# Dense experts' first product by seven block products, in an attention and two mixture-of-experts kernel

## The chip, the core and the metric

The kernel runs on one core of a Trainium2 chip. The core has five engines with queues of their own: TensorE (PE in the profile; its weight loads are PEld), VectorE (DVE), ScalarE (ACT), GpSimd (POOL) and SyncE (SP), which issues most transfers. TensorE multiplies a weight tile of 128 x 128 with up to 512 moving columns and adds into an accumulation bank (PSUM); the other operands lie in on-chip memory (SBUF). Engines wait for each other by semaphores. The metric is the device time of one execution in microseconds.

## What is computed

Attention with rotated positions (2 batches, 8 heads, 576 positions, head size 64) gives x, 1,152 tokens of 512 values. A first layer of 8 experts follows, of which each token takes its two best (routed experts), and then a second layer in which every token goes through all 4 experts (dense experts). The change is in the dense experts:

```python
def _moe2_ref(x, domain_probs, w1, w2) -> np.ndarray:
    N, D = x.shape                       # 1152, 512
    E = w1.shape[0]                      # 4; w1 is E x 512 x 1024, w2 is E x 1024 x 512
    p = domain_probs / (domain_probs.sum(-1, keepdims=True) + 1e-09)
    out = np.zeros((N, D), dtype=np.float32)
    for e in range(E):
        h = np.maximum(x @ w1[e], 0.0)   # the first product
        out += p[:, e:e + 1] * (h @ w2[e])   # the second product
    return out.astype(np.float32)
```

## The kernel before

**Numbers in two parts.** Every large operand is kept as a high part, rounded to the type that TensorE multiplies fast, and a low part, the difference. A product a x b is three products: high x high, low x high and high x low. `wchunk` (L94) loads a weight chunk of 128 x 512 as `raw` (five buffers), lets one engine cast the high part (L99 on ScalarE) and another subtract the low part (L102), both into one tile, `w1c` for first weights and `w2c` for second ones (eight buffers each).

**Stages.** Attention runs to about 190 us, with products of 288 columns (`av`, L392, and `ps_s`, L321). Then the routing is worked out, and the eight routed experts run in the loop at L789, each on up to 320 gathered tokens: first product `ps_h` (L804), ReLU on ScalarE (`hh`, L805), low part on VectorE (`hl`, L806), second product `ps_y` (L866), copy to `yt`, transpose `pt_y` (L835). Outputs are written to `yd` in memory; those of the last expert are added to x2 at once (L841).

**Between the layers.** x2, the dense experts' input, has nine tiles of 128 tokens. For each tile `fetch` (L713) issues two gathers from `yd` on GpSimd's queue (L722), `combine` (L726) adds both to x2 on VectorE (L729), and `turn_x2` (L733) transposes the tile on TensorE (L736) and splits it into `xh2` and `xl2` (L112, L113). The tables `fetch_at` and `combine_at` (L775) put tiles 0 to 2 into the last routed expert; tiles 3 to 8 follow between the first products of the first dense expert, with `raw` buffers for the gathered rows.

**Dense experts.** The loop at L899 takes the four experts in turn. The first product goes by hidden block f (eight of 128) and token group t (three of 384): 12 matmuls of 384 columns into one of three banks (L922), a ReLU into `h2h` on ScalarE (L923) and a low part into `h2l` on VectorE (L924). Then the second product takes 24 matmuls of 512 columns per token tile (L937), and VectorE adds each tile, times its probability, to the accumulator (L940 for the first expert, L942 for the others), which after the last expert leaves by a put on GpSimd's queue (L946). Second weights are loaded and split in the first product, first weights of the next expert in the second one; ScalarE casts and GpSimd subtracts.

**What sets the order.** A scheduler orders the instructions of each engine, largely as they are written; `issue_after` holds one behind another. Each engine then works through its queue in order.

Of the kernel before, what the change touches and what calls it, by code (L numbers as in the profile page):

```python
# [15 lines left out]
P = 128  # L16
# [11 lines left out]
def tile_attention_moe_moe(  # L28
# [65 lines left out]
    def wchunk(src, pool, tag, hi, lo):  # L94
        raw = rawp.tile([P, 512], F32, tag="raw", name="raw")
        nc.sync.dma_start(raw if len(src.shape) == 2 else raw.rearrange("p (k f) -> p k f", k=KC), src)
        t = pool.tile([P, 2, 512], F32R, tag=tag, name=tag)
        if hi is nc.scalar:
# [4 lines left out]
        return t  # L103

    def w1chunk(src, f, hi, lo):
        return wchunk(src[:, f * P:(f + 1) * P].rearrange("(k p) f -> p k f", p=P), w1p, "w1c", hi, lo)
# [400 lines left out]
    psg = ctx.enter_context(tc.tile_pool(name="psg", bufs=3, space=PSUM))  # L507
    psy = ctx.enter_context(tc.tile_pool(name="psy", bufs=2, space=PSUM))
    pstr = ctx.enter_context(tc.tile_pool(name="pstr", bufs=2, space=PSUM))
# [104 lines left out]
    y_writes, y_adds = [], []  # L614
# [98 lines left out]
    def fetch(c):  # L713
        for k2 in range(2):
            i = 2 * c + k2
            if c > 2:
                ygs[i] = rawp.tile([P, DM], F32, tag="raw", name="yg")
            else:
                if i % 3 == 0:
                    yg = gx.tile([P, 3, DM], F32, tag="g", name="yg")  # L720
# [68 lines left out]
    for e in range(E1):  # L789
# [4 lines left out]
        for f in range(FC):  # L794
# [28 lines left out]
            if e == LAST:  # L823
                last_steps(f)
# [6 lines left out]
        def turn_y(d, yt, yn, e=e):  # L831
# [5 lines left out]
            if e == LAST:  # L837
                for j in range(NJ):
                    n = min(P, CAP - j * P)
                    c = NT - full + j if j < full else NT - NJ  # L840
                    y_adds[:] = [vec.scalar_tensor_tensor(  # L841
                        x2[0:n, c, dd], pt[0:n, j * P:(j + 1) * P], tp[0:n, c, 4:5], x2[0:n, c, dd],
                        op0=ALU.mult, op1=ALU.add)]
# [15 lines left out]
        for d in range(KC):  # L859
            for f in (2 * d, 2 * d + 1):  # L860
# [30 lines left out]
    uc1 = {0: wc1}  # L891
# [3 lines left out]
    hh = x2p.tile([P, FC, NT * P], F32R, name="h2h")  # L895
    hl = x2p.tile([P, FC, NT * P], F32R, name="h2l")
    acc = x2
    puts = []
    for e in range(E2):  # L899
        wc1 = uc1.pop(e)  # L900

        if e == 0:
            order = [(f, t, 3) for t in (0, 3, 6) for f in range(FC)]
        else:
            order = [(f, t, 3) for f in range(FC) for t in (0, 3, 6)]
        wc2 = []
        for i, (f, t, m) in enumerate(order):
            if e == 0 and i < 12:
                if i % 2 == 0:
                    with tc.issue_after(y_adds[0].ins):  # L910
                        fetch(i // 2 + 3)
                        combine(i // 2 + 3)
                else:
                    turn_x2(i // 2 + 3)
            if i % (len(order) // FC) == 0:
                wc2.append(w2chunk(u2[e], len(wc2), nc.scalar, nc.gpsimd))
            o = slice(t * P, (t + m) * P)
            ps = psg.tile([P, 512], F32, tag="g1", name="ps_h2")[:, 0:m * P]
            w = wc1[f].rearrange("p s (k f) -> p s k f", k=KC)
            for n, (s, xx, kk) in enumerate(  # L920
                    [(s, xh2, kk) for kk in range(KC) for s in (0, 1)] + [(0, xl2, kk) for kk in range(KC)]):
                nc.tensor.matmul(ps, w[:, s, kk, :], xx[:, kk, o], start=(n == 0), stop=(n == 3 * KC - 1))  # L922
            nc.scalar.activation(hh[:, f, o], ps, AF.Relu)  # L923
            vec.scalar_tensor_tensor(hl[:, f, o], ps, 0.0, _f(hh[:, f, o]), op0=ALU.max, op1=ALU.subtract)  # L924
        if e + 1 < E2:
            uc1[e + 1] = []
        for c in range(NT):
# [82 lines left out]
```

## Time and profile before

| | us |
|---|---|
| median of three runs | 895.47 (893.74 to 895.69) |
| profiled execution | 893.92 |
| its span, from the first to the last instruction | 892.1 |
| attention and routing | about 200 |
| routed experts | about 275, to 475 |
| dense experts | 475 to 884 |

The profile is of one execution. Busy time is that of an engine's instructions; matmuls overlap, so a matmul's duration is longer than the distance to the next one, and it is the distance, or a stretch divided by its matmuls, that gives the price. The granted clock (PEclk) is 1.00 at 2.4 GHz and 0.5 at 1.2 GHz. The chain of waits follows the work that ended last back through what released it.

### The profile page before, as it was taken

What the parts mean: (1) busy time and instruction counts of PE and PEld (TensorE: products, weight loads), DVE (VectorE), ACT (ScalarE), POOL (GpSimd) and SP (SyncE); (2) the same over time, 40 slices, a digit from 0 to 9 for tenths busy, and PEclk for the clock granted to TensorE, in tenths of its full rate; (3) what the DMA queues carried; (4) which work ended last, traced back from release to release, by engine and by line L of the source; (5) the groups of instructions that cost most, each with busy time, mean ns of one, the idle gap of its engine ahead of it and who ended that gap; (6) DMA issues with size and microseconds to landing.
All of it is one profiled execution on the core that took longest, in us unless ns stands there. A gap on an engine that the chain in (4) does not pass through costs nothing. (4 is left out here: it accounts for less than half of the span.)

```text
span 892.1 us, 13550 instructions
## 1 busy us (share of the span) xinstructions
PE 837.3 (94%) x5148; PEld 780.3 (87%) x5148; DVE 409.1 (46%) x796; ACT 345.0 (39%) x771; POOL 343.9 (39%) x299
## 2 busy tenths in 40 slices
PE   4899999938979989999999899999999999999996
PEld 3799999938979989999999898899888998899885
DVE  7988888867455435446566521122111221122111
ACT  3778888734325345446432440033103330032100
POOL 6768774647455425334045340052104220040011
PEclk9999999978999989999999999999999999999998
DMA  5423231617446465465373420041103210010011
GB/s 147 112 69 96 70 82 41 181 56 246 144 136 187 141 200 152 141 215 173 116 220 102 136 80 15 0 119 38 34 1 85 58 36 12 1 36 1 12 48 47
DMA packets 94636, 84.42 MB, mean 95 GB/s; under 512 B 14036, under 2 KB 74852, under 8 KB 94564
## 3 DMA queue, kind: packets, MB, share of 16 engines
q1 hardware_dynamic: 89204, 69.34, 26.8%
q0 software_dynamic: 4384, 13.47, 4.7%
q8 instruction: 43, 0.70, 0.3%
q10 hardware_dynamic: 976, 0.66, 0.2%
q14 instruction: 29, 0.24, 0.1%
HBM read 69.66 MB, written 9.66 MB: 89 GB/s over the span
## 5 line engine op out<-in xcount | busy, mean ns | idle before, releaser
L937 PE MATMUL ps_y<-w2c,h2h 128*128 128x512 f32 (+1 forms) x592 | 182.4, 389 | 0.0
L922 PE MATMUL ps_h<-xh,w1c 128*128 128x384 f32 x768 | 149.8, 337 | 3.1 <-DVE h2l L924 3.1
L102 POOL TENSOR_TENSOR w2c<-raw,w2c 128x512 fp32r<-128x512 f32 x60 | 83.0, 1409 | 164.8 <-ACT w2c L99 164.7
L922 PEld LDWEIGHTS ps_h<-xh,w1c 128*128 128x128 f32 x768 | 134.0, 188 | 4.6 <-DVE h2l L924 4.3
L937 PEld LDWEIGHTS ps_y<-w2c,h2h 128*128 128x128 f32 x592 | 110.2, 188 | 25.3
L102 POOL TENSOR_TENSOR w1c<-raw,w1c 128x512 fp32r<-128x512 f32 x60 | 77.3, 1293 | 130.9 <-ACT w1c L99 127.8
L866 PE MATMUL ps_y<-hh,w2c 128*128 128x320 f32 x512 | 124.8, 323 | 2.0 <-PEq L742 2.0
L99 ACT CAST w2c<-raw 128x512 fp32r<-128x512 f32 x96 | 56.4, 619 | 174.3 <-issue 133.6
L937 PE MATMUL ps_y<-w2c,h2l 128*128 128x512 f32 (+1 forms) x296 | 115.2, 389 | 0.0
L924 DVE SCALAR_TENSOR_TENSOR h2l<-ps_h,h2h 128x384 fp32r<-128x384 f32 x96 | 53.3, 557 | 134.5 <-ACT h2h L923 134.5
L923 ACT ACTIVATE h2h<-ps_h 128x384 fp32r<-128x384 f32 x96 | 47.0, 492 | 122.0 <-PE ps_h L922 121.0
L804 PE MATMUL ps_h<-xh,w1c 128*128 128x320 f32 x512 | 89.4, 317 | 3.1 <-DVE hl L806 3.1
L866 PEld LDWEIGHTS ps_y<-hh,w2c 128*128 128x128 f32 x512 | 90.2, 195 | 2.2 <-issue 2.2
L866 PE MATMUL ps_y<-hl,w2c 128*128 128x320 f32 x256 | 82.0, 320 | 3.2 <-DVE x L729 1.7
L804 PEld LDWEIGHTS ps_h<-xh,w1c 128*128 128x128 f32 x512 | 79.4, 193 | 3.9 <-DVE hl L806 3.6
L922 PE MATMUL ps_h<-xl,w1c 128*128 128x384 f32 x384 | 82.4, 336 | 0.0
L942 DVE SCALAR_TENSOR_TENSOR x<-ps_y,tp,x 128x512 f32<-128x512 f32 (+1 forms) x28 | 20.5, 732 | 129.5 <-PE ps_y L937 129.5
L922 PEld LDWEIGHTS ps_h<-xl,w1c 128*128 128x128 f32 x384 | 67.9, 188 | 0.0
L937 PEld LDWEIGHTS ps_y<-w2c,h2l 128*128 128x128 f32 x296 | 55.6, 188 | 12.6
L99 ACT CAST w1c<-raw 128x512 fp32r<-128x512 f32 x88 | 54.2, 616 | 13.6 <-DMA raw<-in_moe_w_dram 13.0
L866 PEld LDWEIGHTS ps_y<-hl,w2c 128*128 128x128 f32 x256 | 50.1, 196 | 4.0 <-DVE x L729 2.0
L293 DVE TENSOR_REDUCE nm<-ps_s 128x1 f32<-128x576 f32 x64 | 48.2, 753 | 10.9 <-PE ps_s L321 10.3
(213 smaller groups left out, 1367.6 us busy)
## 6 DMA issues: line engine op xcount, KB each, us to landing
raw<-in_moe_w_dram SPq DMA_DIRECT2D x192, 256.0 KB
Cs<-C SPq DMA_DIRECT2D x28, 144.0 KB
yd<-yn SPq DMA_DIRECT2D x7, 512.0 KB
xd<-xp SPq DMA_DIRECT2D x4, 576.0 KB
vv<-in_v_dram SPq DMA_DIRECT2D x8, 256.0 KB
qk<-in_q_dram SPq DMA_DIRECT2D x7, 256.0 KB
qk<-in_k_dram SPq DMA_DIRECT2D x7, 256.0 KB
yd<-yn SPq DMA_DIRECT2D x7, 128.0 KB
```

Of the source, the lines that this page charges most:

```text
L99: hi.copy(t[:, 0, :], raw)
L102: lo.tensor_sub(t[:, 1, :], raw, _f(t[:, 0, :]))
L293: nc.vector.reduce_max(un.nm[:, c:c + 1], ps[:, :, 0:HS], axis=AX.XY, negate=True)
L804: nc.tensor.matmul(ps, w[:, s, kk, :], xx[:, kk, :], start=(n == 0), stop=(n == 3 * KC - 1))
L866: nc.tensor.matmul(ps, wc2[f][:, s, d * P:(d + 1) * P], xx[:, f, :], start=(n == 0), stop=(n == 3 * FC - 1))
L922: nc.tensor.matmul(ps, w[:, s, kk, :], xx[:, kk, o], start=(n == 0), stop=(n == 3 * KC - 1))
L923: nc.scalar.activation(hh[:, f, o], ps, AF.Relu)
L924: vec.scalar_tensor_tensor(hl[:, f, o], ps, 0.0, _f(hh[:, f, o]), op0=ALU.max, op1=ALU.subtract)
L937: nc.tensor.matmul(ps, xx[:, f, c * P:(c + 1) * P], wc2[f][:, s, dd], start=(n == 0), stop=(n == 3 * FC - 1))
L942: vec.scalar_tensor_tensor(acc[:, c, dd], ps, tp[:, c, 8 + e:9 + e], acc[:, c, dd], op0=ALU.mult, op1=ALU.add)
```

## The change

Experts 1 to 3 get their first product by seven block products in place of eight. The contraction (512), the hidden columns (1,024) and the tokens (1,152) are each halved. For hidden block m and its partner m + 4 (a unit), the four blocks of the weights and four of x give seven products of sums of blocks, with a contraction of 256 and 576 tokens, and the four results are sums of these. Each expert is cut into two sets of two units; a set's four hidden blocks go through the second product at once, which so adds to the accumulator twice as often, with half the matmuls each time.

The sums of x (`T1`, `T2`, `T4` in `Th` and `Tl`; `T3` over a quarter of `xh2` and `xl2`) are formed once, on VectorE and ScalarE, in the first dense expert, which keeps the plain first product. The sums of weights are formed per unit by `unit_weights`, four subtractions of low parts and four half-size additions on GpSimd, in the second product before. The products go to three buffers of two banks (`psu`), for which the pools `psg` and `pstr` are closed. The results are put together on VectorE, partly back into those buffers. A class `InOrder` keeps TensorE, VectorE and ScalarE in the written order from the second half of the first dense expert on. The gathers for tiles 4 to 8 go to temporaries of the dense stage (`tmp`, four buffers) in place of `raw`; tile 3 moves into the last routed expert, and the combines there are held behind the last low part (`last_low`).

```diff
@@ fetch, last_steps @@
-            if c > 2:
-                ygs[i] = rawp.tile([P, DM], F32, tag="raw", name="yg")
+            if c > 3:
+                ygs[i] = temp().rearrange("p j t -> p (j t)")[:, 0:DM]
...
-    fetch_at = {3: (0,), 4: (1,), 5: (2,)}
-    combine_at = {7: (0,), 8: (1,), 9: (2,)}
+    fetch_at = {3: (0,), 4: (1,), 5: (2,), 6: (3,)}
+    combine_at = {7: (0,), 8: (1,), 9: (2,), 10: (3,)}
...
         for c in combine_at.get(i, ()):
-            combine(c)
+            with tc.issue_after(last_low[0]):
+                combine(c)
@@ the dense experts; the loop of L893 to L952 is replaced @@
+    def temp():
+        return x2p.tile([P, 2, TQ], F32, tag="tmp", name="tmp", bufs=4)
...
+    def unit_weights(ra, rb):
+        eng = nc.gpsimd
+        lo, hi = slice(0, 256), slice(256, 512)
+        ta, tb = (split_chunk(x, w1p, "w1c", act, eng) for x in (ra, rb))
+        eng.tensor_tensor(rb[:, hi], rb[:, lo], rb[:, hi], op=ALU.add)
+        eng.tensor_tensor(rb[:, lo], ra[:, lo], rb[:, lo], op=ALU.subtract)
+        eng.tensor_tensor(ra[:, lo], rb[:, hi], ra[:, lo], op=ALU.subtract)
+        eng.tensor_tensor(ra[:, hi], ra[:, hi], ra[:, lo], op=ALU.subtract)
+        tc_, td_ = (split_chunk(x, w1p, "w1c", act, eng) for x in (ra, rb))
...
+    def unit(m, blocks, between):
+        def product(a, b):
+            ps = psu.tile([P, 2, 512], F32, tag="u", name="ps_u")[:, :, 0:TQ]
+            w = blocks[a].rearrange("p s (k f) -> p s k f", k=2)
+            bh, bl = B[b]
+            todo = [(w[:, s, kk], xx[:, kk]) for s, xx in ((0, bh), (1, bh), (0, bl)) for kk in range(2)]
+            for n, (x, y) in enumerate(todo):
+                for j in range(2):
+                    pe.matmul(ps[:, j], x, y[:, j * TQ:(j + 1) * TQ], start=(n == 0), stop=(n == len(todo) - 1))
+            return ps
+
+        def add(ps, other, dst=None):
+            dst = ps if dst is None else dst
+            dve.tensor_tensor(dst, ps, other, op=ALU.add)
+            return dst
+
+        p1 = temp()
+        act.copy(p1, product("11", "11"))
+        between()
+        both = add(product("S2", "T2"), p1, temp())
+        c11 = add(product("12", "21"), p1)
+        relu_hi(2 * m, h0, c11)
+        between()
+        relu_lo(2 * m, h0, c11)
+        v = add(product("S1", "T1"), both, temp())
+        p7 = product("S3", "T3")
+        add(p7, both, both)
+        c22 = add(p7, v)
+        relu_hi(2 * m + 1, h1, c22)
+        c12 = add(product("S4", "22"), v)
+        relu_hi(2 * m, h1, c12)
+        relu_lo(2 * m + 1, h1, c22)
+        relu_lo(2 * m, h1, c12)
+        c21 = add(product("22", "T4"), both)
+        relu_hi(2 * m + 1, h0, c21)
+        relu_lo(2 * m + 1, h0, c21)
+
+    def second(e, s, wc2, cs, after=()):
...
+                todo = [(part, xx, f) for f in (0, 1, 3, 2) for part, xx in ((0, hs[0]), (0, hs[1]), (1, hs[0]))]
...
+    def join(c):
+        combine(c)
+        if c + 2 < NT:
+            fetch(c + 2)
...
+        else:
+            nxt = sets[n + 1] if n + 1 < len(sets) else None
+            for m in range(MS):
+                unit(m, units.pop(m), lambda: split_w2(nc.gpsimd))
+                if m == 0:
+                    load_w2(2, nxt)
+            order = [*range(5, NT), *range(5)]
+            second(e, s, w2s[e, s], order, [lambda x=x: [f() for f in x] for x in make])
```

Here `between` casts and subtracts one chunk of second weights; `h0` and `h1` are the token halves. InOrder's operations all carry the line of its helper, L931 in the new file.

TensorE, first product of expert 1, before: the first three of the expert's 24 groups, each of 8 + 4 matmuls (`ps_h` is the accumulation bank).

```order
L922 MATMUL ps_h_13278<-xh_2638,w1c 128x384 x8
L922 MATMUL ps_h_13278<-xl_2639,w1c 128x384 x4
L922 MATMUL ps_h_13293<-xh_2638,w1c 128x384 x8
L922 MATMUL ps_h_13293<-xl_2639,w1c 128x384 x4
L922 MATMUL ps_h_13308<-xh_2638,w1c 128x384 x8
L922 MATMUL ps_h_13308<-xl_2639,w1c 128x384 x4
```

TensorE, the same place now: the seven products of a unit begin with these (`ps_u` is a buffer of two banks, `Th` and `Tl` the parts of the sums of x).

```order
L931 MATMUL ps_u<-xh_2638,w1c 128x288 x8
L931 MATMUL ps_u<-xl_2639,w1c 128x288 x4
L931 MATMUL ps_u<-Th,w1c 128x288 x8
L931 MATMUL ps_u<-Tl,w1c 128x288 x4
L931 MATMUL ps_u<-xh_2638,w1c 128x288 x8
L931 MATMUL ps_u<-xl_2639,w1c 128x288 x4
```

Behind every 12 matmuls of 384 columns stood a ReLU and a low part; now each 12 of 288 columns are one product, and VectorE has this between two sets of accumulations (all eleven operations of a unit are these).

```order
L931 TENSOR_TENSOR tmp<-ps_u,tmp 128x576
L931 TENSOR_TENSOR ps_u<-ps_u,tmp 128x2x288
L931 SCALAR_TENSOR_TENSOR h2l<-ps_u,h2h 128x576
L931 TENSOR_TENSOR tmp<-ps_u,tmp 128x576 x2
L931 TENSOR_TENSOR ps_u<-ps_u,tmp 128x2x288 x2
L931 SCALAR_TENSOR_TENSOR h2l<-ps_u,h2h 128x576 x2
L931 TENSOR_TENSOR ps_u<-ps_u,tmp 128x2x288
L931 SCALAR_TENSOR_TENSOR h2l<-ps_u,h2h 128x576
```

VectorE, the last routed expert, before: combines (`x<-yg`) between the last three low parts (`hl`).

```order
L729 SCALAR_TENSOR_TENSOR x_2634<-yg,tp,x_2634 128x512
L806 SCALAR_TENSOR_TENSOR hl<-ps_h,hh 128x320
L729 SCALAR_TENSOR_TENSOR x_2634<-yg,tp,x_2634 128x512 x2
L806 SCALAR_TENSOR_TENSOR hl<-ps_h,hh 128x320
L729 SCALAR_TENSOR_TENSOR x_2634<-yg,tp,x_2634 128x512 x2
L806 SCALAR_TENSOR_TENSOR hl<-ps_h,hh 128x320
L729 SCALAR_TENSOR_TENSOR x_2634<-yg,tp,x_2634 128x512
L102 TENSOR_TENSOR w1c<-raw,w1c 128x512 x3
L841 SCALAR_TENSOR_TENSOR x_2634<-pt_y,tp,x_2634 128x128 x2
```

VectorE, the same place now.

```order
L818 SCALAR_TENSOR_TENSOR hl<-ps_h,hh 128x320
L108 TENSOR_TENSOR w1c<-raw,w1c 128x512
L818 SCALAR_TENSOR_TENSOR hl<-ps_h,hh 128x320
L740 SCALAR_TENSOR_TENSOR x_2634<-yg,tp,x_2634 128x512 x8
L108 TENSOR_TENSOR w1c<-raw,w1c 128x512
L854 SCALAR_TENSOR_TENSOR x_2634<-pt_y,tp,x_2634 128x128 x2
```

All combines, now eight, stand behind the last low part and ahead of the additions of the transposed output.

## Rows read from the trace of the kernel before

**Rows 1.** The page's busy times: us, share of the span, instructions.
```profile
PE 837.3 (94%) x5148; PEld 780.3 (87%) x5148; DVE 409.1 (46%) x796; ACT 345.0 (39%) x771; POOL 343.9 (39%) x299
```
**Rows 2.** Chain of waits in order of time, dense experts: start us, us, what.
```profile
533.06 50.39 PE ps_y L937 x216
583.45 49.92 PE ps_h L922 x288
```
**Rows 3.** Busy time by stretch, first product of a dense expert.
```profile
core 0: us, PE busy (x) PEld busy (x) DVE busy (x) ACT busy (x) POOL busy (x), PEclk, DMA share, GB/s
583.45:633.37 49.92, 49.92 (x289) 49.92 (x289) 13.50 (x24) 16.36 (x33) 15.01 (x12) 1.00 0.25 73
```
**Rows 4.** Timeline of TensorE in attention: start us, us, engine, line, operation.
```profile
170.90 0.30 PE L321 MATMUL ps_s<-Cs,A 128*128 128x288 f32 x1
171.04 0.31 PE L321 MATMUL ps_s<-C,A 128*128 128x288 f32 x1
171.18 0.31 PE L321 MATMUL ps_s<-Cs,A 128*128 128x288 f32 x1
...
180.68 0.30 PE L392 MATMUL av<-el,v 128*128 128x288 f32 x1
...
181.60 0.29 PE L394 MATMUL av<-e,v 128*128 128x288 f32 x1
```
**Rows 5.** Weight loads under those matmuls: duration ns min/median/max.
```profile
L392 PEld LDWEIGHTS av<-el,v x128: 186/188/192, 30.9 to 183.3; 128*128 128x128 f32 x128
```
**Rows 6.** Groups of instructions, shapes apart: count | busy us, mean ns | idle before.
```profile
L924 DVE SCALAR_TENSOR_TENSOR h2l<-ps_h,h2h 128x384 fp32r<-128x384 f32 x96 | 53.3, 557 | 134.5 <-ACT h2h L923 134.5
L942 DVE SCALAR_TENSOR_TENSOR x<-ps_y,tp,x 128x512 f32<-128x512 f32 x26 | 19.5, 751 | 125.1 <-PE ps_y L937 125.1
L293 DVE TENSOR_REDUCE nm<-ps_s 128x1 f32<-128x576 f32 x64 | 48.2, 753 | 10.9 <-PE ps_s L321 10.3
L923 ACT ACTIVATE h2h<-ps_h 128x384 fp32r<-128x384 f32 x96 | 47.0, 492 | 122.0 <-PE ps_h L922 121.0 <-issue 1.0
L294 ACT ACTIVATE eb<-ps_s,nm 128x576 f32<-128x576 f32 x64 | 47.8, 747 | 7.5 <-DVE nm L293 7.4
```
**Rows 7.** Weight subtractions (L102) by engine: duration ns min/median/max.
```profile
L102 POOL TENSOR_TENSOR w1c<-raw,w1c x60: 1262/1294/1312, 161.8 to 734.8; 128x512 fp32r<-128x512 f32 x60
...
L102 DVE TENSOR_TENSOR w2c<-raw,w2c x36: 681/694/3893, 197.6 to 444.9; 128x512 fp32r<-128x512 f32 x36
```
**Rows 8.** Busy time by stretch, last routed expert: columns of rows 3.
```profile
455.40:458.90 3.50, 3.50 (x23) 3.11 (x22) 2.98 (x5) 0.93 (x2) 2.59 (x4) 1.00 0.69 212
460.90:464.30 3.40, 3.40 (x15) 3.40 (x15) 2.41 (x4) 0.43 (x1) 0.97 (x2) 0.51 0.61 186
```
**Rows 9.** Timeline, end of the routed experts; brackets: idle time before, releaser.
```profile
454.65 0.75 DVE L729 SCALAR_TENSOR_TENSOR x<-yg,tp,x 128x512 f32<-128x512 f32 x1 [2.50 <-DMA yg<-yd,ti]
...
460.11 0.48 DVE L806 SCALAR_TENSOR_TENSOR hl<-ps_h,hh 128x320 fp32r<-128x320 f32 x1
...
460.65 0.42 PE L866 MATMUL ps_y<-hl,w2c 128*128 128x320 f32 x1 [1.72 <-DVE x L729]
...
458.29 0.95 POOL L722 DMA_INDIRECT yg<-yd,ti  x1 [0.30 <-issue]
459.55 1.47 POOL L722 DMA_INDIRECT yg<-yd,ti  x1 [0.30 <-issue]
...
475.38 0.42 PE L922 MATMUL ps_h<-xh,w1c 128*128 128x384 f32 x1
475.87 0.55 PE L835 MATMUL pt_y<-csb,yt 128*128 128x128 f32 x3
```
**Rows 10.** Chain of waits, a gather's flight at the start of the dense experts.
```profile
480.72 3.55 DMA yg<-yd,ti
```
**Rows 11.** The page's group of the dense first product: columns as rows 6.
```profile
L922 PE MATMUL ps_h<-xh,w1c 128*128 128x384 f32 x768 | 149.8, 337 | 3.1 <-DVE h2l L924 3.1
```
**Rows 12.** Chain of waits near the end: a put of output rows.
```profile
851.85 0.96 POOL out_dram L946
```

More of the change, by code (lines that the diff above doesn't have):

```diff
@@ L103, in wchunk, with w1rows @@
         return t
+    def w1rows(src, f):
+        return src[:, f * P:(f + 1) * P].rearrange("(k p) f -> p k f", p=P)
     def w1chunk(src, f, hi, lo):
[L106 removed]
+        return wchunk(w1rows(src, f), w1p, "w1c", hi, lo)
     def w2chunk(src, f, hi, lo):
@@ L859, in tile_attention_moe_moe @@
         for d in range(KC):
-            for f in (2 * d, 2 * d + 1):
+            for f in (2 * d, 2 * d + 1) if e < LAST else (d, d + FC // 2):
                 wc1.append(w1chunk(src1, f, nc.scalar, alternate(f) if e < LAST else vec))
@@ L890, in tile_attention_moe_moe, with __init__, __getattr__, op @@
     mctx.close()
-    uc1 = {0: wc1}
     x2p = ctx.enter_context(tc.tile_pool(name="x2p", bufs=1))
-    hh = x2p.tile([P, FC, NT * P], F32R, name="h2h")
-    hl = x2p.tile([P, FC, NT * P], F32R, name="h2l")
+    TH = NT * P // 2
+    TQ = TH // 2
+    NS = 2
+    MS = FC // 2 // NS
+    def temp():
+        return x2p.tile([P, 2, TQ], F32, tag="tmp", name="tmp", bufs=4)
+    class InOrder:
+        def __init__(self, eng, last=None):
+            self.eng, self.last = eng, last
+        def __getattr__(self, name):
+            def op(*args, **kwargs):
+                with tc.issue_after(self.last) if self.last is not None else ExitStack():
+                    done = getattr(self.eng, name)(*args, **kwargs)
+                if self.last is not None:
+                    self.last = done.ins
+                return done
+            return op
@@ L897, in tile_attention_moe_moe @@
+    act, dve, pe = InOrder(nc.scalar), InOrder(vec), InOrder(nc.tensor)
     acc = x2
     puts = []
[L899 to L927, printed above, removed]
-            if e + 1 < E2 and c < FC:
-                uc1[e + 1].append(w1chunk(u1[e + 1], c, nc.scalar, nc.gpsimd))
-            cuts = (0, 256, 512) if e == E2 - 1 and c == NT - 1 else (0, 512)
@@ new lines, in relu_hi, with relu_lo, plain_chunk @@
+    def relu_hi(f, o, src):
+        hi = hs[0][:, f, o]
+        return act.activation(hi if len(src.shape) == 2 else hi.rearrange("p (j t) -> p j t", j=2), src, AF.Relu)
+    def relu_lo(f, o, src):
+        hi, lo = hs[0][:, f, o], hs[1][:, f, o]
+        if len(src.shape) == 3:
+            hi, lo = (x.rearrange("p (j t) -> p j t", j=2) for x in (hi, lo))
+        return dve.scalar_tensor_tensor(lo, src, 0.0, _f(hi), op0=ALU.max, op1=ALU.subtract)
+    def plain_chunk(f, w, t):
+        o = slice(t * P, (t + 3) * P)
+        ps = psg.tile([P, 512], F32, tag="g1", name="ps_h2")[:, 0:3 * P]
+        w = w.rearrange("p s (k f) -> p s k f", k=KC)
+        for n, (s, xx, kk) in enumerate(
+                [(s, xh2, kk) for kk in range(KC) for s in (0, 1)] + [(0, xl2, kk) for kk in range(KC)]):
+            mm = pe.matmul(ps, w[:, s, kk, :], xx[:, kk, o], start=(n == 0), stop=(n == 3 * KC - 1))
+        return mm, relu_hi(f, o, ps), relu_lo(f, o, ps)
@@ L932, in tile_attention_moe_moe @@
+    def second(e, s, wc2, cs, after=()):
+        last = e == E2 - 1 and s == NS - 1
+        for i, c in enumerate(cs):
+            cuts = (0, 256, 512) if last and i == len(cs) - 1 else (0, 512)
             for d0, d1 in zip(cuts, cuts[1:]):
@@ L952, in tile_attention_moe_moe, with load_w2 @@
                     puts.append(put)
+            for f in after[i:i + 1]:
+                f()
+        return mm, done
+    for c in (4, 5):
+        fetch(c)
+    def join(c):
+        combine(c)
+        if c + 2 < NT:
+            fetch(c + 2)
+    steps = [lambda: turn_x2(3)] + [g for c in range(4, NT) for g in (lambda c=c: join(c), lambda c=c: turn_x2(c))]
+    sets = [(e, s) for e in range(E2) for s in range(NS)]
+    w2s, raws = {}, []
+    def load_w2(n, key):
+        if key in sets:
+            have = w2s.setdefault(key, [])
+            for f in set_chunks(key[1])[len(have):len(have) + n]:
+                raws.append((key, load_raw(u2[key[0]][f * P:(f + 1) * P, :])))
+                have.append(None)
```

128 lines of the change are left out of this document (112 added, 16 removed).

## The prediction

> **What bounds the kernel now.** I read the busy times first: TensorE is at work for 94% of the span, no other engine for half of it [rows 1]. Busy does not mean bound, so the chain of waits comes next. From 533 us on it is one unbroken run of dense products, first product (`ps_h`), second product (`ps_y`), and so on, in pieces of 49.92 us for 288 matmuls and 50.39 us for 216 [rows 2]. The table by stretch says the same: TensorE without a gap, granted clock 1.00, VectorE busy 13.50 us of 49.92, ScalarE 16.36, GpSimd 15.01 [rows 3]. So in these stages a matmul costs its share of the piece: 49.92/288 = 173.3 ns for 384 columns, 50.39/216 = 233.3 ns for 512. Only fewer or cheaper matmuls help there, and the other engines have room. Two places before it are not like that: the last routed expert, and the start of the first dense expert, where TensorE waits for VectorE [rows 9, 11].
>
> **The first product of experts 1 to 3.** A unit is two 128-wide blocks of hidden columns over all 1,152 tokens. Before, that is 2 blocks x 3 token groups x 12 = 72 matmuls of 384 columns: 72 x 173.3 = 12.48 us. Now it is 7 products x 6 pairs of operands x 2 token halves = 84 matmuls of 288 columns, as the order of TensorE shows. The trace has matmuls of this size, in attention: eight that follow each other start at 180.68 to 181.60 us, 0.92/7 = 131 ns apart; where the output changes bank after two, 170.90 to 171.04 is 140 [rows 4]. In the new products the bank changes at every matmul, so the cost lies between 131 and 140. I take 133.3, since the 384-column piece above keeps one bank per 12 and pays the same 13 ns beyond its columns, and keep 140 for the range. Then a unit is 84 x 133.3 = 11.20 us, 1.28 us less; 12 units give 15.4 us (at 140 ns: 11.76 us, 8.6 in all). The Trainium skill, "TensorE: Matmul & The Clock Gate", section Back-to-back issue gap, gives a gap of N/2.4 + 2.5 ns at the high clock; by it the estimate would be 122.5 and 162.5 ns, and the gain 12 x (72 x 162.5 - 84 x 122.5) = 16.9 us. Both rows lie some 11 ns above it, so the rows are used.
>
> **The additions that the seven products need.** Each unit gives VectorE 7 additions and 4 low parts of 576 elements, ScalarE 1 copy and 4 ReLUs. VectorE takes 557 ns for 384 elements, 751 for 512, 753 for a reduction over 576 [rows 6]; I take 0.75 us, so 11 x 0.75 = 8.3 us of 11.2. ScalarE lies between 492 ns (384) and 747 (576, with an exponential): 0.70. That fits in sum, but the order is fixed, so I walked one unit through. Products end at 1.76, 3.36, ... 11.36 us (1.6 apart, the last matmul lasting 0.3). VectorE: sum with P2 to 4.15, c11 5.75, its low part after the ReLU 7.24, v 7.99, P5 into the sum 8.95, c22 9.70, c12 (waits for P6) 10.55, low part of c22 11.3. Only then is the buffer of P5 free, and the first product of the next unit, due at 11.2, needs it, as there are three buffers: it starts about 0.2 us late. The later buffers are free 0.3 us or more before they are needed. Behind a set's second unit comes the second product, with buffers of its own, and its first tiles read the half that is finished first. So I charge 0.2 us x 6 sets = 1.2 us; from 0 (additions at 0.72) to 0.7 us x 6 = 4 (at 0.85; no row shows VectorE writing back into an accumulation buffer, so this end is open).
>
> **Weights, second product, end.** A unit's weights now take GpSimd four subtractions of 1.3 us [rows 7] and four half-size additions, about 0.7 each by half of that: 8 us, two units 16 in a second product of 9 x 2.8 = 25.2 us. Its four second-weight subtractions per set (5 us) lie in 22 us of units. Hidden; the cover is gone only if GpSimd takes 25 us for 16. The second product keeps 216 matmuls of 512 columns per expert; halving the contraction doubles VectorE's accumulations, 0.75 us [rows 6] every 2.8 us: hidden. The last rows leave every 2.8 us instead of every 5.6; a put takes GpSimd 0.96 us [rows 12]: hidden, and what follows the last matmul stays as it is.
>
> **The last routed expert.** Before, VectorE waits 2.50 us at 454.65 for a gathered row, with low parts queued behind it; the last low part comes at 460.11, TensorE waits 1.72 us for it, and then the granted clock is 0.51 for 3.4 us: 15 matmuls there, against 23 in the 3.5 us before [rows 8, 9], some 7 too few, 1.1 us. Now all low parts stand ahead of all eight combines, so this goes: 2.8 us. What is late next: the combines. The last gather is issued at 459.55 and lands some 3.7 us later, so the eighth combine ends at 464.0, one weight subtraction later VectorE adds the first transposed output (465.5), and the second transpose of x2 on TensorE, due at about 464.0, waits for that buffer. I charge 1.5 us. Net 1.3 us gained (from nothing, if the clock falls again, to 2.8).
>
> **The start of expert 0.** Before, TensorE waits 3.1 us there for low parts queued behind combines [rows 11]. Now the gathers for tiles 4 to 8 use buffers that are free only when the last transpose of the routed experts is done, 1.0 us after the dense products start. Four issues 1.26 us apart (459.55 less 458.29), landing 3.55 us or more later [rows 9, 10]: the first half of tile 5 lands at 7.5 us; by VectorE's order it is combined ahead of a low part and the second half of tile 4, which thus ends at 9.5. TensorE reaches the transpose of tile 4 at 7.8 us: 1.7 us of waiting, and 0.3 before the first second product reads the fourth low part. 2.0 instead of 3.1, 1.1 gained; between 3.1 gained and 3 lost, as this is a chain of six handovers. The sums of x for the products (14 per half) lie on VectorE in stages that leave it more than half idle [rows 3]. Those with two operands in on-chip memory can be held up by GpSimd: such a subtraction has a median of 694 ns, and a longest of 3,893 [rows 7]. Eight stand between accumulations in expert 0's second half; each group has 2.8 us and a second buffer, so I charge nothing, 3 us for the range.
>
> **Sum.** 15.4 - 1.2 + 1.3 + 1.1 = 16.6 us. The profiled execution took 893.92 us (span 892.1, 1.8 around it), 1.55 less than the median of the three runs, 895.47. Against it: 877.3; against the median: 878.9. I say 878.
>
> **Rivals.** (a) *A changed bank costs 7 ns each*: gain 8.6 - 1.2 + 2.4 = 9.8, 885 us. For: [rows 4]; against: the step behind it, 171.04 to 171.18, changes no bank and takes 140 as well. (b) *The gathers take back what the units give*: the chain above slips by a landing (4 us) at the start of expert 0, and the clock falls after it as it did before: 883 us. For: such waits stand there now [rows 9, 11]; against: gathers no longer share buffers with weights. (c) *VectorE becomes the bound of the units, and the kernel slower*. Additions that read and write accumulation buffers with GpSimd at work could be held up as the 3,893 ns row was. From 1.15 us per addition (11 x 1.15 = 12.7 us) the unit costs more than it did and the head's gain is gone; at 1.5 us, twice my value, it is 16.5 us and the kernel takes 878 + 12 x 5.2 = 940 us. Against: rows with one operand from an accumulation buffer keep their time, 557 and 751 ns with hardly any spread [rows 6], and every operation of a unit has one. (d) *The weight loads bind*. The load row is busy for all 49.92 us of a first product [rows 3]; each load lasts 188 ns [rows 5]. If loads could not overlap, 84 x 188 = 15.8 us per unit instead of 11.2: 878 + 12 x 4.6 = 933 us. Against: under the 288-column matmuls, 133 ns apart, the loads last 188 ns too [rows 4, 5], so they overlap. The Trainium skill, "Perfetto Trace Analysis", section Identifying the Most-Contended Engine, takes the busy share of loads as the measure of TensorE's headroom, which speaks for this rival; the trace speaks against it. (e) *The change does not do what it says*: excluded, the order has 84 matmuls in each of 12 units.
>
> **Chances and range.** Forecast 0.65 (871 to 882), (a) 0.10, (b) 0.12, something between (a) and no gain, with VectorE at 0.9 to 1.1 us, 0.05; (c) 0.06; (d) 0.02. Range 870 to 887: it holds the forecast, (a) and (b), and ends below at 894 - 15.4 - 2.8 - 3.1 = 872 less the spread of runs. A measurement of this kernel tells 0.2% (1.8 us) from no change. Faster 0.91, same 0.02, slower 0.07.
>
> **What would show it.** In the profile after, products of a unit should start 1.6 us apart and the units of a set take 22.4 to 22.8 us; the 288-column matmuls should be 133 ns apart; VectorE's additions should be near 0.75 us; a wait of 0.2 us should stand ahead of each set's second unit. The wait of 1.72 us should be gone and one of 1.5 stand at the second transpose, one of 1.7 us at tile 4's. I am wrong if additions take over 0.85 us, if the granted clock falls inside the units, or if the first dense expert ends later than before, measured from its start.

## The result, and the profile after

The changed kernel takes 882.4 us in the median of four runs (881.14 to 883.97), against 895.58 us of the kernel before beside it (893.74 to 896.96): a ratio of 0.9855, with a 95% interval of 0.9831 to 0.9879. That is 13.2 us less. The forecast was 878 us, so the direction and most of the size came as said, and the time lies in the range of 870 to 887; but it lies 0.4 us above the 871 to 882 that the forecast itself was given. 3.4 us of the forecast's gain of 16.6, reckoned against the medians, are missing.

The profiled execution took 883.97 us, with a span of 882.2 us, the slowest of the four. The page's first line answers [rows 1]:

```profile
PE 823.6 (93%) x5280; PEld 766.6 (87%) x5280; DVE 513.7 (58%) x932; ACT 365.2 (41%) x791; POOL 396.1 (45%) x359
```

TensorE has 132 matmuls more, and is busy for 13.7 us less; VectorE is busy for 104.6 us more, and in experts 1 to 3 TensorE waits for that work only 0.24 us a set, as will be seen.

I cut both traces at the same five places, by the start of the first matmul of each stage, so that the differences add up to that of the spans:

| from the start | before, us | after, us | difference | forecast |
|---|---|---|---|---|
| to the last routed expert | 440.87 | 440.20 | -0.67 | 0 |
| last routed expert | 34.51 | 35.15 | +0.64 | -1.3 |
| expert 0 | 107.90 | 111.97 | +4.07 | -1.1 |
| experts 1 to 3, to the last matmul | 300.90 | 286.91 | -13.99 | -14.2 |
| behind the last matmul | 7.96 | 7.96 | 0 | 0 |
| span | 892.14 | 882.19 | -9.95 | -16.6 |

So the block products did what was forecast, to 0.2 us, and the two stages ahead of them did the opposite.

**Experts 1 to 3.** The chain of waits, in order of time (start us, us, engine, tile, line, count), answers [rows 2]:

```profile
536.84 25.44 PE ps_h L931 x144
562.29 25.19 PE ps_y L931 x108
587.48 22.64 PE ps_u L931 x168
610.12 25.19 PE ps_y L931 x108
```

A set's two units take 22.64 us where half a first product took 49.92/2 = 24.96 [rows 2]. The second product of a set takes 25.19, half of 50.39: cutting it in two costs nothing. The table by stretch, for the first two units and the second product behind them, with the columns of [rows 3]:

```profile
587.48:610.12 22.64, 22.64 (x169) 22.43 (x169) 14.62 (x21) 7.80 (x13) 5.18 (x4) 1.00 0.17 49
610.12:635.31 25.19, 25.19 (x110) 20.29 (x110) 8.12 (x11) 5.01 (x9) 16.03 (x16) 1.00 0.16 43
```

TensorE is shown busy throughout, the granted clock is 1.00, VectorE is busy 14.62 us of 22.64, and GpSimd's sums of weights take 16.03 us of the second product's 25.19. The groups of VectorE and ScalarE in the units (count, busy us, mean ns, idle before) answer [rows 6]:

```profile
L931 DVE TENSOR_TENSOR ps_u<-ps_u,tmp 128x576 f32<-128x576 f32 x48 | 36.5, 761 | 11.1 <-PE ps_u L931 11.1
L931 DVE SCALAR_TENSOR_TENSOR h2l<-ps_u,h2h 128x576 fp32r<-128x576 f32 x48 | 36.2, 755 | 18.3 <-ACT h2h L931 17.6
L931 DVE TENSOR_TENSOR tmp<-ps_u,tmp 128x576 f32<-128x576 f32 x36 | 27.2, 755 | 22.8 <-PE ps_u L931 22.8
L931 ACT ACTIVATE h2h<-ps_u 128x576 fp32r<-128x576 f32 x48 | 31.4, 653 | 89.6 <-DVE ps_u L931 89.5
```

An addition that writes back into its accumulation buffer takes 761 ns, 6 more than one that writes to on-chip memory; the forecast had 750 for both.

**The start of the dense experts.** TensorE waits twice between 440 and 545 us (engine, tile, line, what it waited for: us in total, times, longest):

```profile
PE pt L747 <- DVE x L740: 4.7, 1, 4.7
PE pt L747 <- DVE x L854: 2.6, 1, 2.6
```

The 1.72 us of [rows 9] and the 3.1 us of [rows 11] are gone, as forecast. In their place stand 2.6 us at the second transpose of x2 (forecast 1.5) and 4.7 us at the transpose of tile 4 (forecast 1.7). About the end of each the granted clock falls; the table by stretch, columns of [rows 3]:

```profile
466.50:469.90 3.40, 3.40 (x15) 3.40 (x14) 0.75 (x2) 0.59 (x1) 0.00 (x0) 0.50 0.18 62
476.00:482.00 6.00, 6.00 (x38) 5.96 (x38) 4.03 (x11) 3.29 (x6) 3.95 (x4) 1.00 0.90 298
487.00:493.80 6.80, 5.71 (x18) 5.43 (x19) 5.10 (x9) 1.08 (x2) 5.08 (x5) 0.50 0.48 139
```

The first and the third stretch are at 0.50, the lower level (1.2 GHz), for 3.4 and 6.8 us; the second begins 1.1 us before the wait ends. TensorE is slower in such a stretch: it has 15 matmuls in the first, where [rows 8] has 23 in 3.5 us at 1.00, and in the third ten matmuls of 384 columns take 3.20 us, 320 ns each in place of 173.3 (the row of the chain of waits below). The middle row is the time in which the gathers should fly: the DMA engines are 90% busy with 298 GB/s, most of it weights.

The timeline of that place (start us, us, engine, line; in brackets the idle time before and what ended it) and two rows of the chain of waits, a flight and the ten matmuls at half clock:

```profile
475.35 0.42 PE L931 MATMUL ps_h<-xh,w1c 128*128 128x384 f32 x1
...
477.13 0.94 POOL L733 DMA_INDIRECT tmp<-yd,ti  x1 [15.97 <-ACT w2c L931]
478.38 1.30 POOL L733 DMA_INDIRECT tmp<-yd,ti  x1 [0.30 <-issue]
479.98 0.95 POOL L733 DMA_INDIRECT tmp<-yd,ti  x1 [0.30 <-issue]
...
482.04 0.75 DVE L740 SCALAR_TENSOR_TENSOR x<-tmp,tp,x 128x512 f32<-128x512 f32 x1 [0.36 <-issue]
486.15 0.75 DVE L740 SCALAR_TENSOR_TENSOR x<-tmp,tp,x 128x512 f32<-128x512 f32 x1 [3.36 <-DMA tmp<-yd,ti]
486.82 0.55 DVE L931 SCALAR_TENSOR_TENSOR h2l<-ps_h,h2h 128x384 fp32r<-128x384 f32 x1
487.29 1.41 DVE L740 SCALAR_TENSOR_TENSOR x<-tmp,tp,x 128x512 f32<-128x512 f32 x2
...
488.08 1.11 PE L747 MATMUL pt<-csb,x 128*128 128x128 f32 x4 [4.75 <-DVE x L740]
```

```profile
479.98 6.14 DMA tmp<-yd,ti
489.20 3.20 PE ps_h L931 x10
```

The dense experts start at 475.35. The third gather, the first half of tile 5, is issued 4.6 us later and lands at 486.13 after a flight of 6.14 us. VectorE has its combine ahead of a low part and of the second half of tile 4, waits 3.36 us for it, and so TensorE's transpose of tile 4 starts at 488.08.

### The profile page after: what moved, and what is told of

Read it like the earlier page. It is cut to its first block, busy times and chain, and to the rows that moved or that the text cites. A ratio compares the mean times of both kernels' runs of the same rounds, so it can differ in the third digit from the quotient of the medians.

```text
span 882.2 us, 14067 instructions
## 1 busy us (share of the span) xinstructions
PE 823.6 (93%) x5280; PEld 766.6 (87%) x5280; DVE 513.7 (58%) x932; ACT 365.2 (41%) x791; POOL 396.1 (45%) x359
## 4 chain that ended last, share of the span: by engine, by line
PE 55%; DMA 2%; issue 2%; POOL 2%; DVE 1%; ACT 0%; POOLq 0%; DVEq 0%; ACTq 0%
PE ps_y L931 21%; PE ps_u L931 15%; PE ps_y L879 7%; PE ps_h L931 5%; PE ps_h L816 5%; DMA raw<-in_moe_w_dram 1%; POOL out_dram L1068 1%; POOL yg L733 1%; PE pt_g L637 1%; DMA tmp<-yd,ti 1%; PE pt_y L848 1%; PE pt L747 0%; DMA yg<-yd,ti 0%; POOL tmp L733 0%; DVE x L740 0%
## 5 line engine op out<-in xcount | busy, mean ns | idle before, releaser
L931 PE MATMUL ps_y<-w2c,h2h 128*128 128x512 f32 (+1 forms) x584 | 183.8, 394 | 0.0
L108 POOL TENSOR_TENSOR w1c<-raw,w1c 128x512 fp32r<-128x512 f32 x84 | 108.7, 1311 | 144.0 <-ACT w1c L931 107.6
L931 PEld LDWEIGHTS ps_y<-w2c,h2h 128*128 128x128 f32 x584 | 109.7, 189 | 25.4
L931 PE MATMUL ps_y<-w2c,h2l 128*128 128x512 f32 (+1 forms) x292 | 114.7, 393 | 0.0
L931 DVE SCALAR_TENSOR_TENSOR x<-ps_y,tp,x 128x512 f32<-128x512 f32 (+1 forms) x64 | 47.5, 743 | 107.4 <-PE ps_y L931 107.4
L816 PEld LDWEIGHTS ps_h<-xh,w1c 128*128 128x128 f32 x512 | 78.6, 191 | 3.3 <-DVE hl L818 3.1
L931 ACT ACTIVATE h2h<-ps_u 128x576 fp32r<-128x576 f32 x48 | 31.4, 653 | 89.6 <-DVE ps_u L931 89.5
L931 PEld LDWEIGHTS ps_y<-w2c,h2l 128*128 128x128 f32 x292 | 55.2, 189 | 12.5
L931 PE MATMUL ps_u<-xh,w1c 128*128 128x288 f32 x384 | 59.4, 297 | 0.0
L931 ACT CAST w1c<-raw 128x512 fp32r<-128x512 f32 x48 | 26.9, 619 | 75.4 <-POOL raw L982 75.4
L931 PEld LDWEIGHTS ps_u<-xh,w1c 128*128 128x128 f32 x384 | 53.9, 188 | 1.8 <-issue 1.3
L108 DVE TENSOR_TENSOR w2c<-raw,w2c 128x512 fp32r<-128x512 f32 x44 | 44.2, 1034 | 19.2 <-ACT w2c L105 19.2
L303 ACT ACTIVATE eb<-ps_s,nm 128x576 f32<-128x576 f32 x64 | 47.8, 747 | 7.7 <-DVE nm L302 7.5
L816 PE MATMUL ps_h<-xl,w1c 128*128 128x320 f32 x256 | 48.5, 311 | 0.0
```

The costliest lines, as they stand in the source:

```text
L303: nc.scalar.activation(e.rearrange("p (a s) -> p a s", a=2), ps[:, :, 0:HS], AF.Exp, bias=un.nm[:, c:c + 1], accum_out=un.rs[:, c:c + 1],)
L816: nc.tensor.matmul(ps, w[:, s, kk, :], xx[:, kk, :], start=(n == 0), stop=(n == 3 * KC - 1))
L931: done = getattr(self.eng, name)(*args, **kwargs)
```

## The experiments

Stage times below are cut as in the table above, from each run's own trace. Ratios are to the kernel before, timed beside it.

**Plain products in the new structure** (`plain_sets`, and once more as `plain_again`). Experts 1 to 3 in two sets, with all else as in the changed kernel, but the sums left out:

```diff
-                unit(m, units.pop(m), lambda: split_w2(nc.gpsimd))
+                for j, wj in enumerate(units.pop(m)):
+                    for t in (0, 3, 6):
+                        plain_chunk(2 * m + j, wj, t)
+                    split_w2(nc.gpsimd)
```

> Experts 1 to 3 get plain first products (four chunks a set, 384 columns) in the structure of the changed kernel: two sets, the same start of expert 0, the same last routed expert; no sums of x or of weights. Theory (the block products are worth 24.96 - 22.64 = 2.32 us in each of six sets, and the new start costs what the trace after shows): the first product of a set takes 24.96 us again, the time is 882.4 + 13.9 = 896.3 us, about 0.7 us above the kernel before. Rival (part of the gain comes from the two sets, or the sums cost time in expert 0): the time is 892 us or less.

Measured: 899.73 us, ratio 1.0046 (1.0012 to 1.0080), 0.5% above the kernel before and 3.4 us above the time expected; the rival, 892 us or less, is out. Experts 1 to 3 took 303.7 us, 16.8 us more than with block products. That is more than the 13.9 expected, and the chain shows it: a set's first product took 25.44 us, not 24.96.

```profile
587.95 25.44 PE ps_h L931 x144
613.39 25.19 PE ps_y L931 x108
```

The difference is in every matmul: 176.7 ns from one to the next on average, where the kernel before has 173.3 (49.92 us for 288, [rows 2]). The same two numbers stand in the changed kernel's own profile, where expert 0's second set takes 25.44. Two repeats were to tell whether that belongs to the program.

> The kernel with plain first products in two sets, a second execution. In the first one its matmuls of 384 columns stood 176.7 ns apart from 513 us on, where the kernel before has 173.3. Theory (the distance is one of two that an execution can fall into): 173.3 ns and a set's first product of 24.96 us in this one, experts 1 to 3 300.8 us. Rival (the distance belongs to the program): 176.7 ns, 25.44 us and 303.7 us again.

> The kernel before, a second execution with a profile. What it tells: how far the stages ahead of the block products differ between executions of one program. Theory (they differ by waits for rows that land early or late, as they did in four executions of the changed kernel's start: 109.1 to 112.0 us for expert 0): expert 0 again 107 to 109 us, last routed expert 34 to 35 us, experts 1 to 3 the same 300.7 us to 0.1 us. Rival (the new start is no slower than the old, only its first profile was): expert 0 109 us or more.

Measured: it belongs to the execution. In this second execution the plain sets take 24.96 us, and in a second one of the kernel before the first products take 50.88 us, 176.7 ns per matmul, where the first one had 49.92. The chains of `plain_again` and of `before_again`:

```profile
585.19 24.96 PE ps_h L931 x144
```

```profile
585.11 50.88 PE ps_h L922 x288
```

With equal distances, experts 1 to 3 take 300.84 us in `plain_again` and 300.90 in the kernel before: two sets and the order written out cost nothing, and the block products gain 300.84 - 286.91 = 13.9 us. In an execution at 176.7 ns they gain 16.8, since neither the matmuls of 288 columns nor those of 512 showed a second distance in any profile here. So the expectation on `before_again` missed in one part: experts 1 to 3 took 303.8 us there and not the 300.7 expected, since the longer distance had not been thought of. Its other part held: last routed expert 34.7 us, and expert 0 108.5 us, 107.6 without the longer distance of its 288 matmuls, against 107.9 in the first profile.

**Loads held back, as written** (`weights_held`). Four loads of weights, needed 50 us later, were written behind the last first product of the first set:

```diff
-                load_w2(1, after)
+                with tc.issue_after(lasts[0].ins):
+                    load_w2(1, after)
```

> The second weights of expert 0's second set (four loads of 256 KB) and all loads behind them are held until the last first product of the first set, so that fewer weights fly while the rows of tiles 4 to 8 are gathered. Theory (the third gather took 6.1 us from issue to landing, against 3.6 in the kernel before, because weight loads share the DMA engines): its flight falls to about 4 us, TensorE's wait of 4.7 us at the transpose of tile 4 to about 2.5, and the stretch at half clock gets shorter; time 878 to 880 us. Rival (the gathers are slow by themselves, four at a time): flight 6 us and wait 4.7 as now, time 882.4 us.

Measured: 881.92 us, ratio 0.9863 (0.9797 to 0.9929). SyncE's queue came out in the same order and its loads flew as before: `issue_after` orders instructions of one engine, and put no wait between TensorE and SyncE. So this says nothing on the theory, and is one more execution of the changed kernel: wait at tile 4 4.3 us, at the second transpose 2.1; expert 0 109.9 us, last routed expert 34.5. `low_twice` and `c22_apart` below have the same start, and give 109.6 and 109.1, 35.6 and 34.0. The first profile, with 112.0, was the slow end of four.

**Loads behind the gathers** (`loads_behind`). The same loads, now into the temporaries that the gathers use (`temp` is the tile that the load goes to), with the next set's loads behind the last of them, `held`, in SyncE's queue:

```diff
-                load_w2(1, after)
+                load_w2(1, after, temp)
...
-                load_w2(1, sets[2])
+                with tc.issue_after(held[0]):
+                    load_w2(1, sets[2])
```

> The four loads of the second weights of expert 0's second set take temporaries that the gathers use before them, and the next set's loads follow them in SyncE's queue, so no weight load flies while the rows of tiles 4 and 5 are gathered (VectorE's order of combines shifts a little with it). Theory (the first gathers share the DMA engines with weights that are not needed yet): the third gather takes 3.6 to 4.5 us from issue to landing instead of 6.1, TensorE's wait at the transpose of tile 4 falls from 4.7 us to 2 or less, expert 0 takes 107 to 109 us instead of 112; time 878 us. Rival (four gathers queue behind each other whatever else flies): flight 5.5 us or more, wait 4 us or more, expert 0 110 us or more.

Measured: 878.37 us, ratio 0.9832 (0.9786 to 0.9878). The DMA engines are 49% busy in the 6 us of the gathers, not 90% (first row of the next fence, a stretch as above). The third gather flies 4.4 us, as the theory said, but VectorE now waits for the second one's flight, which takes 4.98 us: it combines the second half of tile 4 ahead of the first half of tile 5, where the changed kernel does it the other way round. TensorE waits 1.4 us for tile 4, and 2.3 us a little later, at the first second product, for a low part that stands behind the next combine:

```profile
474.00:480.00 6.00, 6.00 (x38) 5.96 (x37) 2.68 (x6) 1.47 (x3) 4.17 (x5) 1.00 0.49 125
```

```profile
475.87 4.98 DMA tmp<-yd,ti
```

```profile
PE pt L747 <- DVE x L854: 3.5, 1, 3.5
PE ps_y L931 <- DVE h2l L931: 2.3, 1, 2.3
PE pt L747 <- DVE x L740: 1.4, 1, 1.4
```

Expert 0 takes 108.8 us, in the 107 to 109 of the theory, but hardly less than the 109.1 to 112.0 of the four executions with the changed kernel's order. This run alone does not separate the loads from VectorE's order, but the two runs with plain products do. They have the order of this run, by the gathers that their combines wait for, and the loads in flight; `plain_again` (the first row as above, then TensorE's waits):

```profile
476.80:482.80 6.00, 6.00 (x38) 5.96 (x38) 3.26 (x10) 3.27 (x6) 4.66 (x4) 1.00 0.93 316
PE ps_y L931 <- DVE h2l L931: 2.3, 1, 2.3
PE pt L747 <- DVE x L740: 0.7, 1, 0.7
```

With the DMA engines 93% busy the wait at tile 4 is 0.7 us (1.0 in `plain_sets`), and the one at the first second product is that of `loads_behind`. So the order turned round is enough to take down the wait of 3.7 to 4.7 us at tile 4, with all loads in flight; that holding them back adds to it is not shown. (The plain runs leave out the sums; `turns_spread` below has the same order with every load and sum, and waits 1.9 us.)

**Transposes spread** (`turns_spread`):

```diff
-    turn_at = {9: (0, 1), 10: (2,)}
+    turn_at = {9: (0,), 10: (1,), 11: (2,)}
```

> One line: of the three transposes of x2 in the last routed expert, the second moves behind the next quarter of its second product and the third behind the one after. Theory (TensorE waits 2.6 us at the second transpose because its buffer is freed by an addition queued behind the eight combines on VectorE, and the 3.4 us at half clock that follow come of that wait): both go, 2.6 + 1.65 = 4.2 us, the dense experts start 4.2 us earlier, time 878.2 us. Rival (VectorE's queue is what is late, and the next transposed output waits as long): the wait moves by one quarter, time 882 us.

Measured: 876.90 us, ratio 0.9813 (0.9734 to 0.9892). The last routed expert takes 32.55 us, 2.6 less than in the changed kernel's profile, where 4.2 were expected, and 1.5 to 3.5 less than in the seven other profiles that have this stage as the changed kernel has it. No stretch between 440 and 545 us is at half clock. Four waits remain, none over 1.9 us:

```profile
PE pt L747 <- DVE x L740: 1.9, 1, 1.9
PE ps_y L931 <- DVE h2l L931: 0.9, 1, 0.9
PE ps_h L931 <- ACT xh L121: 0.7, 1, 0.7
PE pt_y L848 <- DVE x L854: 0.4, 1, 0.4
```

Expert 0 gained too, which was not expected: 106.9 us. The theory held for the place: the second transpose waited for its buffer, and the wait was not moved on. It left out that the order of VectorE in the next stage would shift with the transposes: here too the second half of tile 4 is combined ahead of the first half of tile 5.

**Joins late** (`joins_late`). In expert 0's first set, the combines of tiles 4 and 5 go behind the fourth low part, and the transposes some 5 us back:

```diff
-    steps = [lambda: turn_x2(3)] + [g for c in range(4, NT) for g in (lambda c=c: join(c), lambda c=c: turn_x2(c))]
+    steps = [turn(3), lambda: None, lambda: None, lambda: joins(4, 5), turn(4), turn(5), lambda: joins(6)]
+    steps += [turn(6), lambda: joins(7), lambda: (turn_x2(7), joins(8)), turn(8)]
```

> In expert 0's first set the combines of tiles 4 and 5 stand behind the fourth low part, and the transposes of tiles 4 to 8 some 5 us later in TensorE's order; work, gathers and buffers stay. Theory (the wait of 4.7 us at the transpose of tile 4 is one of place: VectorE holds two low parts behind a row that lands late, and TensorE a transpose that nothing needs yet): the wait goes and the 6.8 us at half clock (3.3 us lost) with it; time 882.4 - 8 = 874.4 us, up to 876 with a wait left. Rival (the gathers themselves are too late for tiles 5 to 8): a wait of 3 to 4 us at a later transpose, time 878 us or more.

Measured: 879.79 us, ratio 0.9835 (0.9771 to 0.9899). Expert 0 takes 103.98 us, the 8.0 us less than in the changed kernel's profile that were expected, and 5.1 less than in the best of the other three (0.5 of the 8.0 is the longer distance in the second set of that profile). No wait is left in it, for later tiles neither; the one of the stage ahead stays:

```profile
PE pt L747 <- DVE x L854: 3.1, 1, 3.1
```

So the loss in expert 0 was one of place, with the same gathers, buffers and flights. The median of the whole time is 2.6 us below the changed kernel's, less than the stage gave, and misses the 874.4 to 876 expected; the stage ahead took 35.65 us here, and the start of the last routed expert lies anywhere from 434.5 to 443.0 us in the profiles of this study, with the same work ahead of it. A part of that spread can be read from the granted clock between 215 us and that start: the four profiles with at most 3.4 us at 0.50 there begin the last routed expert at 434.5 to 435.6 us, the eight with 6.8 to 13.7 us at 436.8 to 443.0. That spread of the routed experts is why stages are compared here and not the whole time alone.

**A low part twice, and a sum put elsewhere** (`low_twice`, `c22_apart`). The forecast says that each set's second unit starts late because the fifth product's buffer comes free with a low part. One run lengthens that, the other takes it away:

```diff
         relu_lo(2 * m + 1, h1, c22)
+        relu_lo(2 * m + 1, h1, c22)
```

```diff
-        c22 = add(p7, v)
+        c22 = add(p7, v, temp())
```

> In each of the 12 units the low part that frees the fifth product's buffer is computed twice, 0.76 us more on VectorE at that place. Theory (the next unit's first product waits 0.24 us for that buffer): in each of six sets this wait becomes 0.24 + 0.76 = 1.0 us, a set's first product takes 23.4 us instead of 22.64, 4.6 us in all; ahead of a second product nothing is added. Rival (the 0.24 us come from something else, as weights or a queue, and VectorE has 2.8 us of room per unit): 22.64 us as before, no change.

> One line: the sum that goes into the fourth quarter's block is written to a temporary and not back into the fifth product's accumulation buffer, which so comes free with that addition and not with the low part behind it. Theory (the buffer is what the next unit waits for): the wait of 0.24 us ahead of each set's second unit goes, a set's first product takes 22.4 us, 1.4 us less in all. Rival (another buffer or an engine is as late): 22.6 us as now.

Measured: experts 1 to 3 take 291.70 us with the low part twice and 285.47 with the sum apart, against 286.91: 4.79 more (4.6 expected) and 1.44 less (1.4 expected). The times were 882.94 us (ratio 0.9899, 0.9852 to 0.9946) and 877.21 us (0.9826, 0.9780 to 0.9872). The chain of `c22_apart`:

```profile
577.76 22.40 PE ps_u L931 x168
600.16 25.19 PE ps_y L931 x108
```

168 matmuls in 22.40 us are 133.3 ns each, with no wait left. In the changed kernel the place reads so (timeline of the end of a set's first unit, VectorE and TensorE):

```profile
596.19 0.76 DVE L931 TENSOR_TENSOR ps_u<-ps_u,tmp 128x576 f32<-128x576 f32 x1
...
597.11 0.77 DVE L931 TENSOR_TENSOR ps_u<-ps_u,tmp 128x576 f32<-128x576 f32 x1 [0.17 <-PE ps_u L931]
597.79 1.57 DVE L931 SCALAR_TENSOR_TENSOR h2l<-ps_u,h2h 128x576 fp32r<-128x576 f32 x2
...
597.98 0.70 PE L931 MATMUL ps_u<-Tl,w1c 128*128 128x288 f32 x4
598.68 0.50 PE L931 MATMUL ps_u<-xh,w1c 128*128 128x288 f32 x2
```

The low parts start at 597.79, behind the addition for P6; the first of the two frees the buffer at about 598.55, and the next unit's first product, due at 597.98 + 4 x 0.133 = 598.51, starts at 598.68; the matmul behind it comes 0.07 us later still, which makes the 0.24.

**All three** (`all_three`): spread transposes, late joins and the sum apart, in one kernel.

> The changed kernel with the spread transposes in the last routed expert, the late joins in expert 0 and the fifth product's sum in a temporary. Theory (the three places do not touch each other): last routed expert 32.5 us, expert 0 104 us, a set's first product 22.4 us; against the changed kernel's profile 2.6 + 8.0 + 1.4 = 12.0 us less, time 870 to 871 us, 0.973 of the kernel before. Rival (the dense experts start 2.6 us earlier and the gathers, released by the last transposes, become late for tiles 5 to 8): expert 0 106 to 108 us, time 873 to 875 us.

Measured: 868.60 us, ratio 0.9728 (0.9694 to 0.9762), 24 us less than the kernel before beside it. Last routed expert 32.35 us, expert 0 104.2, experts 1 to 3 285.47. The waits between 430 and 520 us are these, and no stretch there is at half clock:

```profile
PE ps_h L931 <- ACT xh L121: 0.7, 1, 0.7
PE pt_y L848 <- DVE x L854: 0.2, 1, 0.2
```

The three places do not touch each other, and this version beats both kernels: what the change gave back at the start can be had as well.

## Why the prediction was right, and where it was not

**The block products: right in every term.** The gain without the wait was 300.84 - 285.47 = 15.4 us, as forecast. 133.3 ns per matmul of 288 columns, taken from the lower end of [rows 4], is what `c22_apart` shows to the digit; rival (a), 140 ns for a changed bank, is out, as the bank changes at every one of them. The estimate by the formula of the Trainium skill, "TensorE: Matmul & The Clock Gate", section Back-to-back issue gap, which the section gives for isolated matmuls, was a gain of 16.9 us; against it stand these 15.4, since a matmul of 288 or 384 columns costs 13 ns beyond its columns here and not 2.5. The wait of 0.2 us per set was 0.24, at the buffer that the walk through a unit named, and both runs at that place moved it as the walk says. VectorE's 0.75 us was 0.755 to 0.761, so rival (c) did not come near: `low_twice` shows that a twelfth operation at the worst place of a unit costs its own length, once a set. The weight loads are busy for 22.43 of a set's 22.64 us, and matmuls still come 133.3 ns apart, so rival (d) is out. The Trainium skill, "Perfetto Trace Analysis", section Identifying the Most-Contended Engine, takes the busy share of loads as a measure of TensorE's headroom; the traces do not agree with it here: 168 loads and matmuls now fit into 22.40 us, 7.5 a microsecond, where 288 took 49.92, 5.8 a microsecond, under a load row as full [rows 3].

**The last routed expert: the step "I charge 1.5 us" failed.** The wait of 1.72 us went, and the new one came at the place named, the second transpose of x2 behind the combines. But it took 2.1 to 3.5 us in the eight profiles with this stage, and in six of them the clock fell behind it again, which the forecast had priced only as the lower end of its gain. `turns_spread` shows that the place was the cause.

**The start of expert 0: the step that failed is the chain of handovers.** The forecast let the third gather be issued 3.5 us after the start of the dense experts and land at 7.5; it was issued at 4.6 us (the first at 1.8, not 1.0) and landed at 10.8. So of 3.3 us, 1.1 are late issue and 2.2 the flight, for which I took one row [rows 10], during which the DMA engines were 59% busy. That the weights made it longer is not shown: in `c22_apart`, which has the same start, it is the other way round, issued at 5.9 us, flown in 3.74, landed at 9.6, and the DMA engines were 81% busy in that flight, against 77% in the one of 6.14. What both have in common is VectorE's order, which the forecast had right and let stand: the second half of tile 4 behind a row of tile 5 and a low part. Where the order was turned round, the wait at tile 4 was 0.7 to 1.9 us. What follows the landing was right: 1.9 us to the end of tile 4's second half, forecast 2.0. The wait was 3.7 to 4.7 us instead of 1.7, in all four executions of this order with 3.4 to 6.8 us at half clock about its end, so that a gain of 1.1 us became a loss of 1.2 to 4.1 (at the upper end, with 0.5 us of it from the longer distance of the second set's matmuls). This is rival (b) in its mechanism, a chain that slips and a clock that falls after it, and in its size: it was given 883 us and a chance of 0.12, and 882.4 was measured. The range holds the result because it was drawn to hold this rival too; the forecast's own sum had the two places ahead of the block products wrong, by 1.9 and 5.2 us in the profile.

**Hidden and at the end.** No wait of TensorE stands at the sums of x and of weights, and 7.96 us lie behind the last matmul in both kernels, as forecast.

How much of the measured 13.2 us is due to executions at 176.7 ns per matmul stays open: timed runs leave no trace. An estimate from the matmuls of 384 columns that the kernel before has more: at most 864 x 3.3 ns = 2.9 us, if all runs of one kernel had the one distance and all of the other the other.

## What to carry to other kernels

A product by sums of blocks pays here because TensorE was the only engine without room: count its matmuls by the distance measured for that width, then walk one unit through VectorE with every buffer's release, since a few tenths of a microsecond at a buffer are predictable and can be removed with one temporary. When a change also moves transfers, don't price a new flight by one row: under one start the same gather flew 3.74 and 6.14 us. Look first at what an engine has queued behind the row that may be late, and ask of each wait whether the waiting work is needed there at all: moving transposes and combines a few microseconds back gave more than holding other transfers back. Judge such a change by stages cut at the same matmuls; the whole time carries spreads of stages that it does not touch.

## What the runs showed of the hardware

Matmuls of 384 columns run back to back at one of two distances, 173.3 or 176.7 ns, at a granted clock of 1.00. One program shows both in different executions, and one execution can pass from one to the other: in the changed kernel's profile expert 0 has 173.3 ns at 502 to 511 us and 176.7 from 512 us on. From 515 us to the end of the dense experts each of the twelve profiles keeps one. Widths of 288 (in the block products), 320 and 512 columns showed one distance each (133.3, 146.8, 233.3 ns) in the profiles that have them. What sets it was not found.

Between 440 and 545 us the granted clock fell to 0.50 only about a wait of TensorE, but not about each: waits of 3.0 us in `low_twice` and `c22_apart` at the same transpose were followed by such a stretch in the first and not in the second, and waits of 1.7 and 1.9 us for the last low part of the kernel before were followed by one in both of its profiles. Where no wait was longer than 1.9 us in the new start, as in `turns_spread` and `all_three`, none was seen.
